# Attention decode with a gated feed-forward: w_down with 26 row slots on all partitions, and 256 rows placed apart

## The chip, the cores and the metric

The kernel runs on one core of one Trainium2 chip. The metric is the device time of one execution in microseconds (us). Three executions of the kernel before took 1341.16, 1340.95 and 1341.06 us, a median of 1341.06 us.

## The reference, cut to what matters

Two branches work on the same four vectors `x` (4 x 1024) and are mixed by a gate.

```python
q = (x @ wq)                                   # 4 x 32 heads x 128
scores = einsum("bhqd,bhkd->bhqk", q, k_cache) * 128 ** -0.5
o = einsum("bhqk,bhkd->bhqd", softmax(scores), v_cache)
a = o @ wo                                     # wo: 4096 x 1024
h = silu(x @ w_gate) * (x @ w_up)              # w_gate, w_up: 1024 x 3584
y = h @ w_down                                 # w_down: 3584 x 1024
b = x + sigmoid(x @ w_r) * y
g = sigmoid((x * gate_w).sum(-1))
out = g * a + (1 - g) * b                      # 4 x 1024
```

`k_cache` and `v_cache` hold 4 x 32 x 8192 x 128 values in bf16, 268 MB each. They are read once and used once. With the weights 575.68 MB come out of HBM.

## The kernel before

Everything that is streamed goes through one SBUF tile, `ring`, of 11 units per partition (`flat`, L173). `plan` (L177) is a list, written out by hand, of the place at which each load begins. A load is issued on SyncE's queue (SP) as soon as TensorE has read what stood in its place, so SP's order is the order of the program, and each issue waits for a count of TensorE's matmuls.

The order of the work is: `wq` (queries), `w_gate`, then 32 pairs of K blocks (`k_pair`) and 32 pairs of V blocks (`v_pair`); the V pair d - 8 follows the K pair d. One pair is 8 MB, 64 KB on each partition. VectorE transposes a K pair (L511), TensorE multiplies (L516); after eight K pairs a softmax runs over the scores, GpSimd and ScalarE spread the probabilities out (`spread_p`, L568 and L570), and TensorE multiplies them with the V pairs (L587). `w_up` is loaded and used after the second K pair, and there `h_done` (L375) makes the hidden vector h and turns it so that it can be multiplied with `w_down`. After the last K pair comes `wd_piece` (L404): it loads `w_down` and accumulates its product. Eight V pairs and `wo` follow, in pieces that become smaller towards the end (L681 to L692), and the result is stored.

`w_down` has 3584 rows of 1024 values (2 KB a row), 28 for each of the 128 partitions. Before, 27 of them lie on every partition (`FI = 27`, one transfer, L409, 54 KB a partition). The last 128 rows lie apart: 120 rows on 24 partitions, five rows on each (two transfers, L411, to the partitions 0 to 11 and 32 to 43), and eight rows on eight partitions (L412, 64 to 71). The part of the source for one L411 transfer is three groups of four runs that do not follow each other in memory, because the two transfers take their runs in turn (`e h o s`).

h has to match this placing. Its first 3456 entries (`hT`) come by eight transposes (L382) and eight multiplications (L385). For the rows apart (`hS`), ScalarE brings the entries into the order of the partitions (L392, `hp`), eleven small matmuls turn them (L397, L399), and VectorE multiplies with the gate (L402). `gu_piece` (L364) orders the columns of `w_gate` and `w_up` to match; for the last group of columns it uses two matmuls, of 3 and of 1 columns per row of the placing (L372).

Queues that matter below: SP issues all loads; GpSimd issues none; each transfer is divided among the 16 DMA engines.

Of the kernel before, what the change touches and what calls it, by code (L numbers as in the profile page):

```python
# [112 lines left out]
def kernel(  # L113
# [29 lines left out]
    ND = Bn * H // NQ  # L143
# [5 lines left out]
    FR = 4  # L149
    FG = F // (P * FR)  # L150
    NB = 512
# [10 lines left out]
    const = ctx.enter_context(tc.tile_pool(name="const", bufs=1))  # L162
# [26 lines left out]
    def turned(rows, n, dtype=BF, lo=0):  # L189
        t = TB[tb_turn[0] % 2]  # L190
        tb_turn[0] += 1
        return t[lo:lo + rows, 0:n] if dtype == BF else t[lo:lo + rows, 0:2 * n].bitcast(dtype)

    def load_pair(src, n, cuts=(1, 1), second=None):

        place, down = next(plan)
        lo = place * UN
        if second is None:
            second = place * UN + n if place + 4 <= NU else 0
        at = [lo, second]  # L200
        assert second or (n == RING and lo + n == NU * UN and not down)
        halves = [flat[:, x:x + n] for x in at]
        if cuts == (1, 1) and second == lo + n:
            nc.sync.dma_start(out=flat[:, lo:lo + 2 * n], in_=src)
        else:
            for i, half in enumerate(halves):
                step = n // cuts[i]
                for x in range(0, n, step):
                    nc.sync.dma_start(out=half[:, x:x + step], in_=src[:, i * n + x:i * n + x + step])
        return halves, list(range(RD))[::-1] if down else list(range(RD))  # L210
# [26 lines left out]
    row = const.tile([P, 2, 32], F32)  # L237
    nc.gpsimd.memset(row[:, 0, 0:1], 0.0)
    n = 1
# [19 lines left out]
    for half in range(2):  # L259
        for e in range(2):  # L260
            nc.gpsimd.tensor_copy(out=R[:, 2 * half + e].rearrange("p (n j) -> p n j", n=4),
                                  in_=ident[:, 64 * half + e:64 * half + 64:2].unsqueeze(1).to_broadcast([P, 4, 32]))
# [24 lines left out]
    c12 = const.tile([P, 2, Bn], F32)  # L287
# [32 lines left out]
    TW = DT // 2  # L320


    FI = FG * FR - 1
    FB = P * FI
    SX = 5
    wdv = B_w_down[0:FB].rearrange("(f i) n -> f (i n)", f=P)
    wd_apart = B_w_down[FB:FB + 24 * SX].rearrange("(e h o s) n -> h e o (s n)", e=3, h=2, o=4)
    wd_rest = B_w_down[FB + 24 * SX:F]
    hp = const.tile([P, 2, SX, 3, 4], F32)
    hS = const.tile([72, SX, Bn], BF)  # L330
    cS = const.tile([72, SX, Bn], F32)
    nc.gpsimd.memset(cS[:], 0.0)
    wov = A_wo.rearrange("(g p r) n -> p g r n", p=P, r=FR)

    def x_rows(ps, ws, nb, cols):
# [28 lines left out]
    def gu_piece(view, w_i):  # L364

        ws, _ = load_pair(view.rearrange("(c t) f -> c (t f)", t=DT), TW * F)

        def cols(w, t, i):
            row = w[:, t * F:t * F + FB].rearrange("p (f m) -> p f m", m=FI)
            if i < FG - 1:  # L370
                return [(0, FR, row[:, :, FR * i:FR * i + FR])]
            return [(0, FR - 1, row[:, :, FR * i:FI]), (FR - 1, FR, w[:, t * F + FB:(t + 1) * F])]  # L372
        x_rows(o_ps[w_i], ws, FG, cols)

    def h_done():  # L375
        h = turned(P, 1024, F32).rearrange("p (z n) -> p z n", z=2)
        nc.scalar.activation(out=h, in_=o_ps[0][:], func=ACT.Silu)
        nc.vector.tensor_tensor(out=h, in0=h, in1=o_ps[1][:], op=ALU.mult)
        for z in range(2):
            ht = bank(o_ps[z], 0, [FR, 4, 32])  # L380
            for r in range(FR):
                nc.tensor.transpose(out=ht[:, r].rearrange("p k i -> p (k i)"), in_=h[:, z, r:512:FR], identity=ident[:])  # L382
            kn = min(4, FG - 4 * z)
            for r in range(FR):
                nc.vector.tensor_tensor(out=hT[:, 4 * z:4 * z + kn, r, :], in0=ht[:, r, 0:kn, 0:Bn],  # L385
                                        in1=c12[:, 1:2, :].to_broadcast([P, kn, Bn]), op=ALU.mult)


        strip = slice(32 * ((FG - 1) % 4), 32 * ((FG - 1) % 4) + 32)
        tail = h[strip, 1, FR - 1:NB:FR]  # L390
        for u in range(2):
            nc.scalar.copy(out=hp[strip, u], in_=tail[:, 0:24 * SX].rearrange("p (e h o s) -> p h s e o", e=3, h=2, o=4)[:, u])  # L392
        hs_ps = bank(o_ps[0], 1, [SX, Bn])
        pick = ident[strip, strip.start:strip.start + Bn]
        for u in range(2):
            for v in range(SX):
                nc.tensor.matmul(hs_ps[32 * u:32 * u + 12, v], lhsT=hp[strip, u, v].rearrange("p e o -> p (e o)"), rhs=pick,  # L397
                                 start=True, stop=True, skip_group_check=True)
        nc.tensor.matmul(hs_ps[64:72, 0], lhsT=tail[:, 24 * SX:P], rhs=pick, start=True, stop=True, skip_group_check=True)  # L399
        for lo, m, n in ((0, 12, SX), (32, 12, SX), (64, 8, 1)):  # L400
            nc.gpsimd.tensor_copy(out=cS[lo:lo + m, 0:n], in_=c12[lo:lo + m, 1:2, :].to_broadcast([m, n, Bn]))
        nc.vector.tensor_tensor(out=hS[:], in0=hs_ps[0:72], in1=cS[:], op=ALU.mult)  # L402

    def wd_piece():  # L404
        lo = next(plan)[0] * UN
        assert (FI + SX) * D == 2 * RING and lo + 2 * RING <= NU * UN
        w = flat[:, lo:lo + 2 * RING]
        at = FI * D
        nc.sync.dma_start(out=w[:, 0:at], in_=wdv)  # L409
        for u in range(2):  # L410
            nc.sync.dma_start(out=w[32 * u:32 * u + 12, at:at + SX * D], in_=wd_apart[u])  # L411
        nc.sync.dma_start(out=w[64:72, at:at + D], in_=wd_rest)  # L412
        parts = [(hT[:, i // FR, i % FR, :], w[:, i * D:(i + 1) * D]) for i in range(FI)]
        parts += [(hS[:, v, :], w[0:72, at + v * D:at + (v + 1) * D]) for v in range(SX)]
        for i, (lhsT, rows) in enumerate(parts):
            for n in range(NH):
                mm_acc(n, lhsT, rows[:, n * NB:(n + 1) * NB], start=(i == 0))
# [54 lines left out]
    def flush_sums():  # L472
        while full:
            full.pop(0)()
# [19 lines left out]
    def k_pair(d):  # L494
        g, t = divmod(d, GD)
        Z = Zt[d % 2]
        if d == 0:
            spread(0)
        if t == 0:
            S_ps[g] = S0  # L500
        sps = S_ps[g]
        ks, order = load_pair(kv_view(A_k_cache, d), RING)
        flush_sums()
        for k, n in enumerate(order):
            unit = ks[n // JT][:, (n % JT) * UN:(n % JT + 1) * UN]
            kn = unit.bitcast(U32).rearrange("p (j h i) -> p h j i", j=CJ, h=2)
            T = unit.rearrange("p (j h i e) -> p h j i e", j=CJ, h=2, e=2)
            s = QP - 1 - (RD * t + n)
            for half in range(2):
                step = 2 * k + half  # L510
                nc.vector.transpose(out=kn[:, half], in_=kn[:, half])  # L511
                if step < 2 and ahead:
                    ahead.pop(0)()
                for e in range(2):
                    for z in range(4):
                        nc.tensor.matmul(sps[:, z, :], lhsT=Z[:, 2 * half + e, s:s + P], rhs=T[:, half, 16 * z:16 * z + 16, :, e],  # L516
                                         start=(t + k + half + e == 0),
                                         stop=(t == GD - 1 and k == RD - 1 and half + e == 2))
                if step == RD and d + 1 < ND:
                    spread(d + 1)  # L520
                if step == RD:
                    flush()
                if step == RD + 2:
                    flush_late()
        if t == GD - 1:
            ahead.extend(softmax(g))
            while g > 0 and ahead:
                ahead.pop(0)()
# [199 lines left out]
```

## Time and profile before

| what | value |
|---|---|
| time, median of three runs | 1341.06 us |
| span of the profiled execution | 1339.2 us |
| the rest of the time, outside the span (median less span) | 1.9 us |
| mean granted TensorE clock | 0.901 |
| HBM read | 575.68 MB, 430 GB/s over the span |
| share of the span in which DMA packets of SP's queue ran (16 engines) | 99.6% |
| TensorE, VectorE, ScalarE, GpSimd busy | 77%, 48%, 4%, 5% |
| w_down: main transfer issued | 1111.0 us |
| first matmul with w_down | 1141.33 us, after 5.55 us of waiting for the transfer |
| store of the result issued | 1336.83 us |

The span is counted from the first instruction to the last. The profile has no execution time of its own for this execution beside its span; the median of the runs less the span is 1.9 us, and what is worked out on the span is carried over to the median unchanged. The busy share of an engine is of little use here: with the DMA engines at 99.6%, an engine that waits is waiting for data.

### The profile page before, as it was taken

What the parts mean: (1) busy time and instruction counts of PE and PEld (TensorE: products, weight loads), DVE (VectorE), ACT (ScalarE), POOL (GpSimd) and SP (SyncE); (2) the same over time, 40 slices, a digit from 0 to 9 for tenths busy, and PEclk for the clock granted to TensorE, in tenths of its full rate; (3) what the DMA queues carried; (4) which work ended last, traced back from release to release, by engine and by line L of the source; (5) the groups of instructions that cost most, each with busy time, mean ns of one, the idle gap of its engine ahead of it and who ended that gap; (6) DMA issues with size and microseconds to landing.
All of it is one profiled execution on the core that took longest, in us unless ns stands there. A gap on an engine that the chain in (4) does not pass through costs nothing.

```text
span 1339.2 us, 6936 instructions
## 1 busy us (share of the span) xinstructions
PE 1031.3 (77%) x4654; PEld 139.8 (10%) x1486; DVE 638.7 (48%) x385; ACT 57.7 (4%) x58; POOL 67.0 (5%) x174
## 2 busy tenths in 40 slices
PE   2386787887777788777787977777797778687887
PEld 0011000001010010101001110100111011111111
DVE  2285998556553436555352556634345556100001
ACT  0000000100010000100010000100000000110000
POOL 2000000100010000100010000100001000100000
PEclk9697998898888998888889988888998889689999
DMA  9999999999999999999999999999999999999998
GB/s 415 433 437 437 435 437 435 420 438 433 433 435 437 427 433 435 429 438 431 433 431 433 435 439 427 429 433 435 438 430 428 433 429 429 438 429 445 422 422 352
DMA packets 13032, 576.14 MB, mean 430 GB/s; under 512 B 1436, under 2 KB 1700, under 8 KB 1970
## 3 DMA queue, kind: packets, MB, share of 16 engines
q1 hardware_dynamic: 12994, 575.69, 99.6%
q8 instruction: 24, 0.39, 0.1%
q14 instruction: 6, 0.05, 0.0%
q10 hardware_dynamic: 8, 0.00, 0.0%
HBM read 575.68 MB, written 0.01 MB: 430 GB/s over the span
## 4 chain that ended last, share of the span: by engine, by line
DMA 67%; PE 22%; DVE 9%; POOL 0%; ACT 0%; issue 0%; SPq 0%
DMA ring<-in_A_k_cache_dram 53%; PE S_ps L516 15%; DMA ring<-in_A_v_cache_dram 10%; DVE ring L511 9%; PE o_ps L587 5%; DMA ring<-in_B_w_gate_dram 3%; DMA ring<-in_A_wo_dram 2%; PE o_ps L342 1%; POOL PB L570 0%; DVE mx L536 0%; PE led L633 0%; ACT TB L545 0%; PE acc L296 0%; POOL Z L492 0%; PE o_ps L633 0%
## 5 line engine op out<-in xcount | busy, mean ns | idle before, releaser
L511 DVE STREAM_TRANSPOSE ring<-ring 128x2048 uint32<-128x2048 uint32 x256 | 566.5, 2276 | 307.7 <-DMA ring<-in_A_k_cache_dram 307.7
L516 PE MATMUL S_ps<-ring,Z 128*128 128x512 bf16 x2048 | 519.9, 408 | 229.3 <-DVE ring L511 216.1
L587 PE MATMUL o_ps<-ring,PB 128*64 128x512 bf16 x2048 | 457.4, 384 | 35.7 <-DMA ring<-in_A_v_cache_dram 33.3
L516 PEld LDWEIGHTS <-Z 128*128 128x128 bf16 x512 | 53.0, 104 | 683.0 <-issue 683.0
L617 DVE SCALAR_TENSOR_TENSOR OS<-o_ps,mE,OS 128x512 f32<-128x512 f32 x33 | 24.8, 751 | 161.7 <-ACT OS L613 160.2
L587 PEld LDWEIGHTS <-PB 128*64 128x64 bf16 x512 | 56.7, 111 | 428.3 <-issue 427.6
L625 DVE SCALAR_TENSOR_TENSOR OS<-o_ps,mE,OS 128x512 f32<-128x512 f32 x5 | 3.7, 750 | 143.6 <-ACT OS L623 143.6
L492 POOL COPY Z<-qa 32x4 bf16<-32x4 bf16 x128 | 25.8, 201 | 716.7 <-PE S_ps L516 689.6
L570 POOL COPY PB<-PT 32x1024 bf16<-32x1024 bf16 (+3 forms) x23 | 33.4, 1452 | 466.6 <-PE o_ps L587 360.7
L613 ACT ACTIVATE OS<-o_ps,mE 128x512 f32<-128x512 f32 x11 | 7.6, 687 | 671.2 <-PE o_ps L587 671.2
L568 ACT COPY PB<-PT 32x1024 bf16<-32x1024 bf16 (+3 forms) x21 | 30.3, 1444 | 22.4 <-PE o_ps L587 17.4
L545 ACT ACTIVATE TB<-S_ps,mx 128x2048 bf16<-128x2048 f32 x4 | 7.9, 1967 | 321.7 <-DVE mx L542 321.7
L254 PE MATMUL S_ps<-identb,x 6*128 6x6 bf16 x8 | 0.6, 196 | 22.3 <-DMA x<-in_gate_w_dram 22.3
L342 PE MATMUL o_ps<-ring,xw 128*4 128x512 bf16 (+2 forms) x128 | 12.9, 490 | 3.5 <-DMA ring<-in_B_w_gate_dram 3.5
L633 PEld LDWEIGHTS o_ps<-selg,OS 128*128 128x128 f32 x88 | 11.5, 191 | 8.8 <-issue 8.5
L550 DVE STREAM_TRANSPOSE PT<-TB 128x2048 bf16<-128x2048 bf16 x4 | 9.2, 2312 | 6.4 <-ACT TB L545 6.4
L296 PE MATMUL acc<-ring,hT 128*4 128x512 bf16 x54 | 7.9, 466 | 5.5 <-DMA ring<-in_B_w_down_dram 5.5
L536 DVE TENSOR_REDUCE mx<-S_ps 128x1 f32<-128x2048 f32 x4 | 9.1, 2282 | 6.0 <-PE S_ps L516 6.0
L296 PE MATMUL acc<-ring,LT 128*4 128x512 bf16 x64 | 8.8, 378 | 3.3 <-DMA ring<-in_A_wo_dram 2.8
L633 PE MATMUL o_ps<-selg,OS 128*128 128x8 f32 x88 | 10.5, 245 | 0.0
L623 ACT ACTIVATE OS<-o_ps,mE 128x512 f32<-128x512 f32 x5 | 3.4, 687 | 151.2 <-PE o_ps L587 151.2
L256 DVE COPY xw<-S_ps 128x48 bf16<-128x48 bf16 x1 | 0.2, 184 | 17.5 <-PE S_ps L254 17.5
(83 smaller groups left out, 88.4 us busy)
## 6 DMA issues: line engine op xcount, KB each, us to landing
ring<-in_A_v_cache_dram SPq DMA_DIRECT2D x7, 4096.0 KB
ring<-in_A_k_cache_dram SPq DMA_DIRECT2D x6, 4096.0 KB, 33.9
ring<-in_A_v_cache_dram SPq DMA_DIRECT2D x6, 2048.0 KB, 28.9
ring<-in_B_w_gate_dram SPq DMA_DIRECT2D x1, 7168.0 KB
ring<-in_B_w_up_dram SPq DMA_DIRECT2D x1, 7168.0 KB
ring<-in_B_w_down_dram SPq DMA_DIRECT2D x1, 6912.0 KB
ring<-in_A_wo_dram SPq DMA_DIRECT2D x2, 2048.0 KB
ring<-in_A_wo_dram SPq DMA_DIRECT2D x3, 1024.0 KB, 34.5
```

Of the source, the lines that this page charges most:

```text
L296: nc.tensor.matmul(acc(n), lhsT=lhsT, rhs=rhs, start=start, stop=True, skip_group_check=True)
L342: nc.tensor.matmul(ps[32 * k:32 * k + Bn, z, :].rearrange("p (f r) -> p f r", r=FR)[:, :, lo:hi], lhsT=xT[TW * half + t], rhs=rhs, start=( ...
L492: nc.gpsimd.tensor_copy(out=Z[at, :, QP - 1 + QP * q], in_=qa[at, :, h0 + q, b])
L511: nc.vector.transpose(out=kn[:, half], in_=kn[:, half])
L516: nc.tensor.matmul(sps[:, z, :], lhsT=Z[:, 2 * half + e, s:s + P], rhs=T[:, half, 16 * z:16 * z + 16, :, e], start=(t + k + half + e == 0) ...
L536: nc.vector.tensor_reduce(out=mx[:, 0:1], in_=sps[:].rearrange("p z n -> p (z n)"), axis=AX.X, op=ALU.max)
L550: nc.vector.transpose(out=PT[:].rearrange("p j i -> p (j i)"), in_=PTs)
L568: nc.scalar.copy(out=Bv[at, :, :, q, :], in_=Pv[at])
L570: nc.gpsimd.tensor_copy(out=Bv[at, :, :, q, :], in_=Pv[at])
L587: nc.tensor.matmul(o_ps[w // 2][row:row + NM, w % 2, :], lhsT=PB[:, RD * (d % NW) + n, z].rearrange("p w s j -> p (w s j)"), rhs=vn[:, j0 ...
L617: nc.vector.scalar_tensor_tensor(out=OS[:], in0=o_ps[w // 2][:, w % 2, :], scalar=mE[:, w:w + 1], in1=OS[:], op0=ALU.mult, op1=ALU.add)
L633: nc.tensor.matmul(oT, lhsT=OS[:, q * Dh:(q + 1) * Dh], rhs=selg[:, q].rearrange("p t s -> p (t s)"), start=(q == 0), stop=(q == 3), skip_ ...
```

## The change

Of the 28 rows that fall to a partition, 26 instead of 27 are placed on every partition (`FI = FG * FR - 2`). So 256 rows lie apart instead of 128, in a list `apart`, whose entries are first partition, e, o, rows per partition, and queue:

- partitions 0 to 11, six rows each (72 rows), and 32 to 43, five rows each (60 rows), on SP's queue;
- partitions 64 to 77, one row each (14), 88 to 95, six rows each (48), 12 to 25, one row each (14), and 120 to 127, six rows each (48), on GpSimd's queue.

GpSimd issued no transfer before. Each source is now a run of rows that follow each other in memory, seen as `(e o s)`. In the built program the transfers stand as 12x6144 and 12x5120 on SP, and 14x1024, 8x6144, 14x1024 and 8x6144 on GpSimd; before they stood as 12x1x5120 (twice) and 8x1024 on SP.

The loads are taken out of `wd_piece` into `wd_load`, which is called in the last K pair just after that pair's own load. SP's order stays as it was. On GpSimd the four transfers come after the copies of L492 for the last K pair and before the copies of L570 for the last softmax.

`hS` now has all 128 partitions and six places, with zeros where no row lies. `h_done` takes a second buffer of TB, clears 768 values on 32 partitions of it on GpSimd, and has seven copies on ScalarE instead of two, 24 small matmuls instead of eleven, and no copies of the gate on GpSimd. The products with the rows apart read 128 partitions instead of 72, in six steps instead of five; 26 and 6 make the same 32 steps as 27 and 5.

```diff
-    FI = FG * FR - 1
+    FI = FG * FR - 2
     FB = P * FI
-    SX = 5
+    FT = F - FB
+    SX = 6
-    wd_apart = B_w_down[FB:FB + 24 * SX].rearrange("(e h o s) n -> h e o (s n)", e=3, h=2, o=4)
-    wd_rest = B_w_down[FB + 24 * SX:F]
-    cS = const.tile([72, SX, Bn], F32)
+    apart = [(0, 3, 4, 6, nc.sync), (32, 3, 4, 5, nc.sync), (64, 14, 1, 1, nc.gpsimd), (88, 2, 4, 6, nc.gpsimd),
+             (12, 14, 1, 1, nc.gpsimd), (120, 2, 4, 6, nc.gpsimd)]
...
-            return [(0, FR - 1, row[:, :, FR * i:FI]), (FR - 1, FR, w[:, t * F + FB:(t + 1) * F])]
+            n = FI - FR * i
+            return [(0, n, row[:, :, FR * i:FI]), (n, FR, w[:, t * F + FB:(t + 1) * F].rearrange("p (r f) -> p f r", f=P))]
...
+        hx = turned(P, FT + P * SX, F32)
+        nc.gpsimd.memset(hp, 0.0)
+        nc.scalar.copy(out=tail.rearrange("p (r f) -> p r f", f=P), in_=...)
+        for lo, e, o, s, _ in apart:
+            nc.scalar.copy(out=hp[:, lo // 32, 0:s, lo % 32:lo % 32 + e * o], in_=...)
...
+    def wd_load():
...
         nc.sync.dma_start(out=w[:, 0:at], in_=wdv)
-        for u in range(2):
-            nc.sync.dma_start(out=w[32 * u:32 * u + 12, at:at + SX * D], in_=wd_apart[u])
-        nc.sync.dma_start(out=w[64:72, at:at + D], in_=wd_rest)
+        x = FB
+        for lo, e, o, s, queue in apart:
+            src = B_w_down[x:x + e * o * s]
+            src = src if s == 1 else src.rearrange("(e o s) n -> e o (s n)", e=e, o=o)
+            queue.dma_start(out=w[lo:lo + e * o, at:at + s * D], in_=src)
+            x += e * o * s
...
         ks, order = load_pair(kv_view(A_k_cache, d), RING)
+        if d == ND - 1:
+            wd_load()
```

More of the change, by code (lines that the diff above doesn't have):

```diff
@@ L320 @@
     TW = DT // 2
-    FI = FG * FR - 1
+    FI = FG * FR - 2
     FB = P * FI
-    SX = 5
+    FT = F - FB
+    SX = 6
     wdv = B_w_down[0:FB].rearrange("(f i) n -> f (i n)", f=P)
-    wd_apart = B_w_down[FB:FB + 24 * SX].rearrange("(e h o s) n -> h e o (s n)", e=3, h=2, o=4)
-    wd_rest = B_w_down[FB + 24 * SX:F]
-    hp = const.tile([P, 2, SX, 3, 4], F32)
-    hS = const.tile([72, SX, Bn], BF)
-    cS = const.tile([72, SX, Bn], F32)
-    nc.gpsimd.memset(cS[:], 0.0)
+    apart = [(0, 3, 4, 6, nc.sync), (32, 3, 4, 5, nc.sync), (64, 14, 1, 1, nc.gpsimd), (88, 2, 4, 6, nc.gpsimd),
+             (12, 14, 1, 1, nc.gpsimd), (120, 2, 4, 6, nc.gpsimd)]
+    assert sum(e * o * s for _, e, o, s, _ in apart) == FT
+    hS = const.tile([P, SX, Bn], BF)
     wov = A_wo.rearrange("(g p r) n -> p g r n", p=P, r=FR)
@@ L389, in h_done @@
         strip = slice(32 * ((FG - 1) % 4), 32 * ((FG - 1) % 4) + 32)
-        tail = h[strip, 1, FR - 1:NB:FR]
-        for u in range(2):
-            nc.scalar.copy(out=hp[strip, u], in_=tail[:, 0:24 * SX].rearrange("p (e h o s) -> p h s e o", e=3, h=2, o=4)[:, u])
+        hx = turned(P, FT + P * SX, F32)
+        tail, hp = hx[strip, 0:FT], hx[strip, FT:FT + P * SX].rearrange("p (j s m) -> p j s m", j=4, s=SX)
+        nc.gpsimd.memset(hp, 0.0)
+        nc.scalar.copy(out=tail.rearrange("p (r f) -> p r f", f=P), in_=h[strip, 1].rearrange("p (f r) -> p r f", r=FR)[:, FR - FT // P:FR])
+        x = 0
+        for lo, e, o, s, _ in apart:
+            nc.scalar.copy(out=hp[:, lo // 32, 0:s, lo % 32:lo % 32 + e * o], in_=tail[:, x:x + e * o * s].rearrange("p (m s) -> p s m", s=s))
+            x += e * o * s
         hs_ps = bank(o_ps[0], 1, [SX, Bn])
         pick = ident[strip, strip.start:strip.start + Bn]
-        for u in range(2):
+        for j in range(4):
             for v in range(SX):
[L397 to L404, printed above, removed]
+                nc.tensor.matmul(hs_ps[32 * j:32 * j + 32, v], lhsT=hp[:, j, v], rhs=pick, start=True, stop=True, skip_group_check=True)
+        nc.vector.tensor_tensor(out=hS[:], in0=hs_ps, in1=c12[:, 1:2, :].to_broadcast([P, SX, Bn]), op=ALU.mult)
+    wd = []
+    def wd_load():
         lo = next(plan)[0] * UN
@@ L407, in wd_piece @@
         w = flat[:, lo:lo + 2 * RING]
+        wd.append(w)
         at = FI * D
         nc.sync.dma_start(out=w[:, 0:at], in_=wdv)
-        for u in range(2):
-            nc.sync.dma_start(out=w[32 * u:32 * u + 12, at:at + SX * D], in_=wd_apart[u])
-        nc.sync.dma_start(out=w[64:72, at:at + D], in_=wd_rest)
+        x = FB
[3 more added lines that the diff above has]
+            queue.dma_start(out=w[lo:lo + e * o, at:at + s * D], in_=src)
+            x += e * o * s
+    def wd_piece():
+        w = wd[0]
+        at = FI * D
         parts = [(hT[:, i // FR, i % FR, :], w[:, i * D:(i + 1) * D]) for i in range(FI)]
-        parts += [(hS[:, v, :], w[0:72, at + v * D:at + (v + 1) * D]) for v in range(SX)]
+        parts += [(hS[:, v, :], w[:, at + v * D:at + (v + 1) * D]) for v in range(SX)]
         for i, (lhsT, rows) in enumerate(parts):
```

## The prediction

> **What bounds the kernel now.** I read the page's queues first, then transfers by stretch of time, then the timeline around w_down, then the last microseconds.
>
> ```profile
> span 1339.2 us, 6936 instructions
> DMA  9999999999999999999999999999999999999998
> q1 hardware_dynamic: 12994, 575.69, 99.6%
> q8 instruction: 24, 0.39, 0.1%
> SPq L204 <- PE S_ps L516: 572.6, 29, 26.2
> ```
>
> SP's queue (q1) keeps the 16 DMA engines busy for 99.6% of the span. SP's waits show that loads wait for TensorE to free the ring; but in the trace every load up to the last is issued at least 3.4 us before the first engine has finished the one ahead of it, so no engine runs dry. The end is therefore the end of the last of 16 DMA engines, and a change counts by what it adds to or takes from the latest ones. q8 fetches instructions, 24 times 16 KB.
>
> The stretch from 1330 us to 1340 us, in slices of 0.25 us:
>
> ```profile
> DMA  9999976966668766554541000000000000100000
> q1 hardware_dynamic: 623, 1.51, 38.4%
> ```
>
> The digits fall from 9 to 4 between 1331 and 1335.5 us: the engines don't finish together. The landing records of the last wo transfer give all 16 ends: four engines at 1331.24 to 1331.93, four at 1334.20 to 1334.76, eight at 1335.57 to 1335.98 us. After the last, 3.2 us remain to the span's end (matmul, cast, store), which the change leaves alone. Were all engines level, they would end some 1.6 us earlier (mean of the 16 ends against 1335.98), which caps the gain of any redistribution.
>
> What one engine does in a unit of time, from two stretches of 1.9 us (30.4 engine-us), the first without an instruction fetch, the second with one:
>
> ```profile
> q1 hardware_dynamic: 11, 0.72, 87.6%
> ```
> ```profile
> q1 hardware_dynamic: 15, 0.98, 121.2%
> q8 instruction: 1, 0.02, 3.3%
> ```
>
> Eleven packets of 64 KB take 26.6 us, 2.42 us each, 0.038 us a KB. With a fetch, the 15 packets take 36.8 us instead of 36.3, and the fetch 1.0 us, though 16 KB are worth 0.61. So a visit to another queue costs its engine 1.55 us, 0.94 beyond its bytes. The landings agree: around three fetches the engine concerned falls back by 1.54 to 1.56 us against the others.
>
> Around w_down:
>
> ```profile
> 1111.00 0.33 SPq L409 DMA_DIRECT2D ring<-in_B_w_down_dram  x1
> 1113.16 1.61 SPq L411 DMA_DIRECT2D ring<-in_B_w_down_dram  x2
> 1114.82 0.44 SPq L412 DMA_DIRECT2D ring<-in_B_w_down_dram  x1
> ```
> ```profile
> 1067.12 0.96 POOL L492 COPY Z<-qa 32x4 bf16<-32x4 bf16 x4 [37.69 <-PE S_ps L516]
> 1143.54 4.88 POOL L570 COPY PB<-PT 32x768 bf16<-32x768 bf16 x3 [75.46 <-DVE PT L550]
> ```
> ```profile
> 1141.33 7.95 PE L296 MATMUL acc<-ring,hT 128*4 128x512 bf16 x54 [5.55 <-DMA ring<-in_B_w_down_dram]
> ```
>
> Landing records tell on how many engines a transfer runs: each L411 transfer (three groups of four runs) landed on three, L412 (eight rows) on eight, the load of x (four rows) on four. The main transfer landed on seven engines at 1136.4 to 1137.1 us and on nine at 1139.5 to 1141.3. L411's three are among the seven early ones: they took its 80 KB (3 us) and thereby joined the late. Four early engines were left, and they are the four that end first.
>
> **The change, part by part.**
>
> *Main transfer, 26 slots:* 8 rows of 2 KB less on every engine, -16 KB, -0.60 us on all.
>
> *The rows apart on SP.* The intention reads (3 groups, 4 partitions): three engines. But the source runs now follow each other, and the built program has 12 rows of 6144 and of 5120 elements, with no groups. By the rows for L412 and x (as many engines as rows) each goes to 12 engines, 12 + 10 = 22 KB on each. Twelve of 16 engines cannot avoid the eight that end last: at least four of these get it, +0.83 us. The three that carried 80 KB get 58 KB less, which nobody needs. L412 falls away: -2 KB on eight engines.
>
> *The rows apart on GpSimd:* 248 KB, by the same rows on 14, 8, 14 and 8 engines; which ones no row shows. An engine gets 0 to 28 KB, 15.5 on average. A sum by bytes for a late engine: -16 - 1 (half of L412's 2) + 22 + 15.5 = about +20 KB, +0.8 us; bounds +3 to +34 KB, so +0.1 to +1.3.
>
> *The second queue.* In the stretch of these transfers the engines run nothing but q1 before; now each of the four GpSimd transfers turns up on an engine that is in the middle of q1's packets. No row shows GpSimd's queue. Bounds: 0, if the engine slips the other packet in as smoothly as the next of its own (these start within some ns of the one before); 0.94 us a visit, as for a fetch, which is the only second queue that the trace shows beside q1, and so the value I take. Visits: 14 + 8 + 14 + 8 = 44 over 16 engines, 2.75; an engine that is late and unlucky has three (four at most). 3 x 0.94 = +2.8 us. GpSimd issues the four one after another and the engines' packets then last 1.2 us (32 KB), so I count the visits apart; two that fall together would save 0.94.
>
> *GpSimd's wait.* The first and second issue wait for TensorE as L409 and L411 do (1111 to 1113 us). Behind them on GpSimd stands L570, which starts at 1143.54. Four issues of 1 to 2 us (SP takes 0.3 to 0.9; my estimate is double) end by 1121: 22 us to spare. The data is needed at 1141, behind the main transfer. 0 us; without this cover L570 would delay the first V pair.
>
> *SP's issues:* three instead of four after the K load, 9 to 23 us ahead of need: 0.
>
> *h_done,* at 104 to 108 us:
>
> ```profile
> 107.68 0.17 DVE L402 TENSOR_TENSOR hS<-o_ps,cS 72x20 bf16<-72x20 f32 x1 [0.35 <-PE o_ps L399]
> 115.22 6.70 DVE L511 STREAM_TRANSPOSE ring<-ring 128x2048 uint32<-128x2048 uint32 x3 [7.37 <-DMA ring<-in_A_k_cache_dram]
> ```
>
> Five more ScalarE copies at 0.25 us (two took 0.49), the first longer, 13 more matmuls of some 0.04 us, a clearing on GpSimd under 1 us that can run earlier: +2 to +3 us, inside the 7.37 us in which VectorE waits for the third K pair. 0. Without that cover, up to 3 us in the loads' lead of 9 us, still 0.
>
> *gu_piece* has as many matmuls of the same 512 columns; *wd_piece* has the same 64 matmuls, of which twelve instead of ten read the rows apart: 0, for TensorE waits for data on both sides (5.55 us before, 9.46 after).
>
> Sum: +0.8 + 2.8 = **+3.6 us**. Span 1339.2 + 3.6 = 1342.8; with the 1.9 us outside it 1344.7 us.
>
> **Rivals.**
>
> *Smooth change of queue (not slower).* Place: the engines at 1112 to 1120 us. If a visit costs only bytes, the end moves by +0.1 to +1.3: 1341.9. For it: packets within q1 follow without a gap, and GpSimd's are small (2 and 12 KB). Against: q8. It decides from under 0.63 us a visit at three visits, (2.7 - 0.8) / 3. Measurements of this kernel tell about 0.2% (2.7 us) from no change. [...]
>
> *The placing works as it reads (faster).* 88 KB on three early engines and 96 KB on two more early ones, whose 4 us of lead cover 80 KB more (3.0 us); all others lose 16 KB and take 4: -12 KB, -0.45 us, 1340.6. Against: the merged sources. It needs smooth visits too.
>
> *More visits.* If each GpSimd transfer also visits every engine for its completion, apart from its data, an engine has up to seven visits: 6.6 + 0.8 = +7.4, 1348.5. Against: SP's transfers on fewer engines show landings only on these. [...]
>
> *Fetches.* 13 more matmuls shift TensorE's code; one fetch more or on another late engine is 1.55 us either way. It stays in the range.
>
> **How the numbers follow.** Forecast (two to four full visits, +2.7 to +5.1 with the bytes) 0.50; smooth visits 0.31; placing as it reads 0.07; more visits 0.12. Predicted 1344.7. The range reaches from 1341.2 (smooth, least bytes, 1341.06 + 0.1) to 1347.1 (five visits and 1.3 us of bytes, +6.0), leaving out the placing and most of the last case; the forecast's own is 1343.8 to 1346.2. Slower by over 0.2% (above 1343.74): the forecast and the last, 0.61 after a little off for its lower edge and a little on for an unlucky fetch. Faster by over 0.2% would need 2.7 us where level engines would give 1.6: 0.02. Within: 0.37.
>
> **What would show it.** GpSimd's queue as a line of its own in the list of queues, and its four issues near 1111 to 1121 us. L419 on SP landing on 12 engines; if on three, my reading of the merged source is wrong. q1 packets of 3 instead of 2.42 us next to GpSimd's, if visits cost; if they keep 2.42, the forecast falls to +0.8. The last landing at 1339 to 1340 us instead of 1335.98, all engines shifted alike by the visits, and the four early ones still early. The first w_down matmul at 1143 to 1145 us. VectorE's third K pair still waiting for its load. Wrong also if the loads' lead of 3.4 us is used up somewhere, or if the queue of GpSimd costs time at the start.

## The result, and the profile after

| | median of five runs | lowest and highest |
|---|---|---|
| before | 1341.16 us | 1340.95 to 1341.31 |
| after | 1349.89 us | 1349.03 to 1350.64 |

The ratio is 1.0064 (95% interval 1.0052 to 1.0075): 8.7 us slower. The direction was forecast, the size was not: 1344.7 us was predicted, with a range up to 1347.1. The profiled execution took 1349.03 us, 1.9 us more than its span. It is the fastest of the five: its span is 7.9 us longer than that of before, and this is what the account below explains. No trace shows where the further 0.8 us of the median come from.

The page of the changed kernel, first the span, then how busy the DMA engines were in 40 slices, what they moved, and the queues:

```profile
span 1347.1 us, 6996 instructions
...
DMA  9999999999999999999999999999999999999998
GB/s 416 450 431 421 432 437 434 431 432 434 436 432 434 436 431 432 429 434 436 434 428 436 436 434 431 428 432 432 429 433 435 434 427 366 422 422 439 433 417 338
...
q1 hardware_dynamic: 12996, 575.44, 99.4%
...
q0 software_dynamic: 128, 0.25, 0.1%
```

GpSimd's queue has a line of its own, q0, with 128 packets and 0.25 MB. The row of busy tenths shows nothing at all: it is nine in every slice but the last, as before. The row of GB/s below it does: the 34th slice (1111 to 1145 us) has 366 GB/s, where its neighbours have 427 and 422. The engines' digit is 9 there as well, but they move less.

The timeline around the transfers and the points that the prediction named (start, duration, engine, line, what, in brackets the idle time before it and what ended it):

```profile
109.90 0.18 DVE L404 TENSOR_TENSOR hS<-o_ps,c 128x24 bf16<-128x24 f32 x1 [1.69 <-PE o_ps L403]
115.04 4.50 DVE L525 STREAM_TRANSPOSE ring<-ring 128x2048 uint32<-128x2048 uint32 x2 [4.96 <-DMA ring<-in_A_k_cache_dram]
...
1110.17 0.33 SPq L414 DMA_DIRECT2D ring<-in_B_w_down_dram  x1
1110.88 0.64 POOL L419 DMA_DIRECT2D ring<-in_B_w_down_dram  x1 [43.00 <-PE o_ps L601]
1112.76 0.73 SPq L419 DMA_DIRECT2D ring<-in_B_w_down_dram  x2
1113.03 1.54 POOL L419 DMA_DIRECT2D ring<-in_B_w_down_dram  x3 [1.51 <-PE o_ps L601]
...
1147.53 7.30 PE L296 MATMUL acc<-ring,hT 128*4 128x512 bf16 x52 [6.50 <-DMA ring<-in_B_w_down_dram]
1148.79 4.88 POOL L584 COPY PB<-PT 32x768 bf16<-32x768 bf16 x3 [34.22 <-DVE PT L564]
```

GpSimd has issued its four transfers by 1114.57 us and waits 34 us before its next copies; `hS` is done at 110 us and VectorE still waits 4.96 us for the third K pair. Neither is late. The first matmul with w_down starts at 1147.53 us, 6.2 us later than before.

Where the time went is told by the transfers in two stretches of time. Before, 1111 to 1132 us and then 1132 to 1150 us:

```profile
DMA packets 246, 9.20 MB, mean 438 GB/s; under 512 B 25, under 2 KB 25, under 8 KB 25
...
DMA packets 184, 7.79 MB, mean 433 GB/s; under 512 B 30, under 2 KB 30, under 8 KB 38
```

The same two stretches of the changed kernel:

```profile
DMA packets 343, 7.65 MB, mean 364 GB/s; under 512 B 109, under 2 KB 109, under 8 KB 137
...
q1 hardware_dynamic: 215, 7.39, 97.3%
q0 software_dynamic: 128, 0.25, 4.9%
...
DMA packets 175, 6.62 MB, mean 368 GB/s; under 512 B 40, under 2 KB 40, under 8 KB 40
...
q1 hardware_dynamic: 174, 6.61, 102.5%
```

(The share of a queue adds up the time of all packets that start in the stretch, over the time of 16 engines, so it can exceed 100%.)

In the first, beside GpSimd's packets, 1.55 MB less were moved, worth 3.5 us at 0.438 MB a us. In the second no packet of GpSimd's queue is left, and still 1.17 MB are missing, 2.7 us. This second hole lies where SP's two transfers to the rows apart run. Beyond their bytes (+0.83 us) no term of the prediction stood for it.

The packet records allow a finer count. An undisturbed packet costs 2.42 us per 64 KB; what a packet takes beyond that, summed over the data packets of SP's and GpSimd's queues and divided by 16, is the **excess** per engine. It is used for all runs below.

- Before: 0.06 us per engine in the first stretch, 0.12 in the second.
- After: 3.7 us in the first (53.4 engine-us in SP's packets, 6.1 in GpSimd's own). Some 85 of SP's packets are stretched: packets of 32 KB, worth 1.21 us, take up to 1.6 us longer.
- After: 3.2 us in the second (50.7 engine-us, 64 packets; 64 KB packets take up to 2.7 us longer).

3.7 + 3.2 and the predicted 0.8 us of bytes make 7.7 us. The last landing of the last wo transfer moved by 7.8 us, from 1335.98 to 1343.80 us, the first from 1331.24 to 1337.72 us. In order of their ends the 16 engines finished 5.6 to 7.9 us later, 6.8 us on average. Both kernels move the same bytes in all, so the average is lost time, and it is the excess (6.9 us, less the 0.2 us of before): no engine ran dry for long.

### The profile page after: what moved, and what is told of

Its sections match the earlier page's. It is cut to its first block, busy times and chain, and to the rows that moved or that the text cites. A ratio compares the mean times of both kernels' runs of the same rounds, so it can differ in the third digit from the quotient of the medians.

```text
span 1347.1 us, 6996 instructions
## 1 busy us (share of the span) xinstructions
PE 1040.4 (77%) x4680; PEld 143.2 (11%) x1512; DVE 638.7 (47%) x385; ACT 59.0 (4%) x63; POOL 69.0 (5%) x175
## 4 chain that ended last, share of the span: by engine, by line
DMA 67%; PE 22%; DVE 10%; ACT 0%; issue 0%; SPq 0%; DVEq 0%
DMA ring<-in_A_k_cache_dram 52%; PE S_ps L530 15%; DMA ring<-in_A_v_cache_dram 11%; DVE ring L525 10%; PE o_ps L601 5%; DMA ring<-in_B_w_gate_dram 3%; DMA ring<-in_A_wo_dram 2%; PE o_ps L342 1%; PE led L647 0%; DVE OS L631 0%; DVE mx L550 0%; ACT TB L559 0%; PE acc L296 0%; DVE OS L639 0%; ACT OS L637 0%
## 5 line engine op out<-in xcount | busy, mean ns | idle before, releaser
L530 PE MATMUL S_ps<-ring,Z 128*128 128x512 bf16 x2048 | 525.6, 412 | 225.8 <-DVE ring L525 217.9
L584 POOL COPY PB<-PT 32x1024 bf16<-32x1024 bf16 (+3 forms) x23 | 33.4, 1450 | 428.4 <-PE o_ps L601 363.5
L342 PE MATMUL o_ps<-ring,xw 128*4 128x512 bf16 (+1 forms) x128 | 12.8, 461 | 4.6 <-DMA ring<-in_B_w_gate_dram 4.6
```

Source lines behind the costliest of these rows:

```text
L342: nc.tensor.matmul(ps[32 * k:32 * k + Bn, z, :].rearrange("p (f r) -> p f r", r=FR)[:, :, lo:hi], lhsT=xT[TW * half + t], rhs=rhs, start=( ...
L584: nc.gpsimd.tensor_copy(out=Bv[at, :, :, q, :], in_=Pv[at])
```

## The experiments

Two theories stood at first. **The queue** (Q): an engine that turns to GpSimd's queue and back loses time, as the prediction had it. **Crowding** (C): engines that write into partitions that other engines are writing at the same moment slow each other, whichever queue brings the packet. No record tells which engine writes which partitions of a large transfer; where an expectation says that engines serve or own partitions, that is part of C, assumed by the author and not shown. SP's second hole speaks against Q as the only cause; the first hole fits both.

**e1: all six transfers on SP's queue.**

```diff
-    apart = [(0, 3, 4, 6, nc.sync), (32, 3, 4, 5, nc.sync), (64, 14, 1, 1, nc.gpsimd), (88, 2, 4, 6, nc.gpsimd),
-             (12, 14, 1, 1, nc.gpsimd), (120, 2, 4, 6, nc.gpsimd)]
+    apart = [(0, 3, 4, 6, nc.sync), (32, 3, 4, 5, nc.sync), (64, 14, 1, 1, nc.sync), (88, 2, 4, 6, nc.sync),
+             (12, 14, 1, 1, nc.sync), (120, 2, 4, 6, nc.sync)]
```

> The changed kernel with all six transfers of rows apart on SP's queue; placing, sources and arithmetic as in the changed kernel, which is 8.7 us slower than the one before. Its trace has two stretches in which SP's packets take longer than their size explains: 1113 to 1132 us beside GpSimd's transfers (3.7 us for each engine) and 1137.5 to 1148 us, where SP's own two transfers of rows apart run and no GpSimd packet is left (3.2 us for each engine). Theory Q (the second queue costs): the first stretch goes, the kernel is 4 to 5 us slower than before. Theory C (crowding: a transfer whose engines are more than those that serve its partitions in a 128-partition transfer holds these engines up): the rows of the two 8x6144 transfers crowd as before, only on SP, so it stays 6 to 8 us slower, and packets after the main w_down transfer are stretched by 5 to 7 us for each engine.

Measured: 1348.56 us against 1341.28, ratio 1.0056 (1.0041 to 1.0071). There is no q0, and the slowness stays. It has moved: the first stretch is clean, the second holds all of it, because SP's transfers run behind the main one.

```profile
DMA packets 248, 9.13 MB, mean 435 GB/s; under 512 B 25, under 2 KB 25, under 8 KB 25
...
DMA packets 230, 5.05 MB, mean 281 GB/s; under 512 B 84, under 2 KB 84, under 8 KB 112
...
q1 hardware_dynamic: 228, 5.03, 102.6%
```

The excess is 0.06 us per engine and then 6.8, as much as both holes of the changed kernel together (6.9). Which queue carries the rows does not matter; Q falls as the main cause.

**e2: the kernel before, with the sources of its two transfers merged.** The 60 rows of each L411 transfer follow each other in memory, and so the three groups vanish, as they do in the change. Slots, queue and target partitions stay those of before.

```diff
-    wd_apart = B_w_down[FB:FB + 24 * SX].rearrange("(e h o s) n -> h e o (s n)", e=3, h=2, o=4)
+    wd_apart = [B_w_down[FB + 12 * SX * u:FB + 12 * SX * (u + 1)].rearrange("(e o s) n -> e o (s n)", e=3, o=4) for u in range(2)]
...
-            nc.scalar.copy(out=hp[strip, u], in_=tail[:, 0:24 * SX].rearrange("p (e h o s) -> p h s e o", e=3, h=2, o=4)[:, u])
+            nc.scalar.copy(out=hp[strip, u], in_=tail[:, 12 * SX * u:12 * SX * (u + 1)].rearrange("p (e o s) -> p s e o", e=3, o=4))
```

> The kernel before; only the two transfers L411 take their 60 rows as one run of memory each, so that the built source has 12 rows instead of 3 groups of 4, and the order of the entries of h follows. GpSimd has no transfer. By bytes, twelve engines get 20 KB (0.76 us) and three lose 60 KB: +0.8 us. Theory C: 12 engines write to the partitions 0 to 11 and 32 to 43, which three engines serve in the main transfer: +0.8 and about 3 us more, 3.5 to 4.5 us slower than before, with stretched packets of 10 KB and of the main transfer's end. Theory Q: no second queue, +0.8 us, no packet stretched.

Measured: 1345.7 us, ratio 1.0033 (1.0021 to 1.0046), so +4.4 us from the order of rows in memory alone. Each transfer landed on twelve engines instead of three; so not every transfer is divided among all 16 engines (before, the main transfer landed on 16, each L411 transfer on three, L412 on eight). The second stretch has the hole, though q1 is the only queue with data:

```profile
DMA packets 188, 6.87 MB, mean 382 GB/s; under 512 B 48, under 2 KB 48, under 8 KB 56
...
q1 hardware_dynamic: 187, 6.85, 102.4%
```

The excess is 2.6 us per engine. With the 0.8 us of bytes that makes the 3.3 us by which the profiled execution is longer (a span of 1342.5 us against 1339.2); it is the fastest of six, 1.3 us below their median. The same 24 partitions get the same bytes from twelve engines instead of three; theory C puts the excess down to that.

**e3: the kernel before, with four small transfers on GpSimd's queue** (14 rows of 256 bytes each, into a tile that is not read any more; all else as before).

```diff
+        if d == ND - 1:
+            for i in range(4):
+                nc.gpsimd.dma_start(out=spare[32 * i:32 * i + 14], in_=B_w_down[14 * i:14 * i + 14, 0:128])
```

> The kernel before, with four transfers more, on GpSimd's queue, of 14 rows of 256 bytes each into 14 partitions of a tile that is no longer used; they are issued at about 1068 us and nobody waits for them. They leave the placing of w_down alone and add 14 KB in all. Theory Q: each engine is visited by each transfer, for data and for the completion: as in the changed kernel's first stretch, 3 to 4 us slower (0.94 us for each of 4 visits). Theory C: next to nothing is moved, so at most 0.5 us slower.

Measured: 1341.43 us against 1341.28, ratio 1.0 (0.9991 to 1.001). The transfers of 1068 to 1092 us:

```profile
DMA packets 304, 10.50 MB, mean 438 GB/s; under 512 B 144, under 2 KB 144, under 8 KB 144
...
q1 hardware_dynamic: 176, 10.49, 101.2%
q0 software_dynamic: 128, 0.01, 0.4%
```

128 packets of q0, as many as in the change, and none of SP's packets is stretched. Turning to the second queue costs nothing that can be measured; the 0.94 us a visit is refuted.

**e4: the changed kernel, with SP's two transfers again as three groups** (their source rows lie 44 apart, so they can't merge); GpSimd's stay.

```diff
-    apart = [(0, 3, 4, 6, nc.sync), (32, 3, 4, 5, nc.sync), (64, 14, 1, 1, nc.gpsimd), (88, 2, 4, 6, nc.gpsimd),
-             (12, 14, 1, 1, nc.gpsimd), (120, 2, 4, 6, nc.gpsimd)]
+    apart = [(0, 3, 4, 6, nc.sync, 0, 44, 0), (32, 3, 4, 5, nc.sync, 0, 44, 24), (64, 14, 1, 1, nc.gpsimd, 132, 1, 0),
+             (88, 8, 1, 6, nc.gpsimd, 146, 6, 0), (12, 14, 1, 1, nc.gpsimd, 194, 1, 0), (120, 8, 1, 6, nc.gpsimd, 208, 6, 0)]
...
+            src = B_w_down[FB + x:FB + x + e * g].rearrange("(e k) n -> e k n", e=e)[:, off:off + o * s]
```

> The changed kernel; only the two SP transfers of rows apart take their rows in three groups of 44 (24 for the first, 20 for the second), so that the built source keeps three groups and each transfer should land on three engines, 88 KB on each. GpSimd's four transfers as in the changed kernel. Theory C: the second stretch (3.2 us for each engine) goes, and 0.8 us of bytes on the late engines: 4 to 5 us slower than before. Theory Q: only the bytes go, 7 to 8 us slower than before.

Measured: 1345.41 us, ratio 1.003 (1.0019 to 1.0041): half of the loss is gone. Both transfers landed on three engines. The hole beside GpSimd's packets stays, SP's is closed:

```profile
DMA packets 340, 7.47 MB, mean 356 GB/s; under 512 B 109, under 2 KB 109, under 8 KB 137
...
DMA packets 180, 8.02 MB, mean 446 GB/s; under 512 B 22, under 2 KB 22, under 8 KB 22
```

The excess is 4.0 and 0.08 us per engine (SP's packets alone have 3.6 in the first, the figure that later expectations use). So the two holes are separate and add up.

**e5: GpSimd's two large transfers in groups as well** (two groups of four partitions; the rest as in e4).

```diff
-             (88, 8, 1, 6, nc.gpsimd, 146, 6, 0), (12, 14, 1, 1, nc.gpsimd, 194, 1, 0), (120, 8, 1, 6, nc.gpsimd, 208, 6, 0)]
+             (88, 2, 4, 6, nc.gpsimd, 160, 48, 0), (12, 14, 1, 1, nc.gpsimd, 146, 1, 0), (120, 2, 4, 6, nc.gpsimd, 160, 48, 24)]
```

> The changed kernel with groups kept in all four large transfers of rows apart: three groups on SP as in e4_groups_sp, and two groups of four partitions for the two 8x6144 transfers of GpSimd (rows of 48, 24 for each transfer). [...] Theory C (crowding): the stretch of 3.6 us for each engine beside GpSimd's transfers shrinks to under 0.5 us, and the kernel is between 0.5 us faster and 0.7 us slower than before. Theory C-HBM (engines that read neighbouring rows at the same time are slow, whatever they write): GpSimd's two groups read 12 KB runs that lie 48 rows apart, so it improves too, and this run can't tell it from C. Theory G (GpSimd's queue with large rows costs, crowded or not): still 3 to 4.5 us slower, as e4_groups_sp.

Measured: 1345.31 us against 1341.07, ratio 1.0031 (1.002 to 1.0042). A miss: no better than e4.

```profile
DMA packets 397, 8.38 MB, mean 399 GB/s; under 512 B 152, under 2 KB 152, under 8 KB 180
...
q0 software_dynamic: 166, 0.19, 3.0%
```

399 GB/s is better than 356, but not the 438 of before: an excess of 2.5 us per engine, and 0.4 more behind 1132 us, where GpSimd's packets go on. There are 180 packets of four bytes instead of 84, and the 12 KB packets don't come as eight together any more: the first eight start in four pairs, the others singly, 1.2 to 1.5 us apart. This reads as if GpSimd executed each of the two transfers in four pieces (3 pieces more, 2 transfers and 16 engines make the 96 further packets). Grouping did not act on GpSimd's queue (2.5 us left of e4's 4.0) as on SP's (0.08 us left of 3.2 in e4). Which engines ran the pieces, and into which partitions, the records don't show; so e5 decides nothing between the theories.

**e6: e1's six transfers, with target partitions four apart,** so that no small set of neighbouring partitions is filled.

The list is that of first partition, step, partitions, rows and queue:

```diff
+    apart = [(0, 4, 12, 6, nc.sync), (1, 4, 12, 5, nc.sync), (2, 4, 14, 1, nc.sync), (64, 4, 8, 6, nc.sync),
+             (3, 4, 14, 1, nc.sync), (65, 4, 8, 6, nc.sync)]
...
+            queue.dma_start(out=w[lo:lo + step * (m - 1) + 1:step, at:at + s * D],
+                            in_=B_w_down[x:x + m * s].rearrange("(m s) n -> m (s n)", s=s))
```

> The kernel of e1_all_sp (six merged transfers, all on SP, on 12, 12, 14, 8, 14 and 8 engines, the same rows of the source read in the same way), but the destinations lie four partitions apart: 0, 4, ... 44 and so on, instead of next to each other. Theory C (crowded destinations): the stretch of packets, 6.8 us for each engine in e1_all_sp, falls to 0.5 to 2 us, and the kernel is 1 to 3 us slower than before instead of 7.3. Theory C-HBM (neighbouring rows read by many engines): nothing changes, 7 us slower.

Measured: 1359.78 us, ratio 1.0137 (1.0123 to 1.0151). The time can't be used: the spaced targets made the last K pair's work wait for these transfers.

```profile
1143.04 17.66 DVE L527 STREAM_TRANSPOSE ring<-ring 128x2048 uint32<-128x2048 uint32 x8 [38.68 <-DMA ring<-in_B_w_down_dram]
1145.40 12.86 PE L532 MATMUL S_ps<-ring,Z 128*128 128x512 bf16 x48 [25.16 <-DVE ring L527]
```

VectorE waited 38.68 us for w_down's transfers before it could go on with the last K pair, TensorE stood still for 25.16 us, the next V load was issued at 1151 instead of 1123 us, and the DMA engines ran dry (only 2.60 MB between 1132 and 1150 us). The excess fell from e1's 6.8 to 0.8 us per engine, which fits crowding, but with no V load beside the transfers it is no proof. A spaced placing without that wait was not tried.

**e7: the kernel before, with the 27th slot of all 128 partitions on GpSimd's queue:** 256 KB, about as much as the change gives to it, but spread over all partitions.

```diff
-        nc.sync.dma_start(out=w[:, 0:at], in_=wdv)
+        nc.sync.dma_start(out=w[:, 0:at - D], in_=wdv[:, 0:at - D])
...
+            nc.gpsimd.dma_start(out=wd[0][:, (FI - 1) * D:FI * D], in_=wdv[:, (FI - 1) * D:FI * D])
```

> The kernel before; only the 27th row slot of all 128 partitions (128 rows, 256 KB) is taken out of the main transfer and loaded by one transfer of GpSimd's queue, issued after the last K pair's load. [...] Theory C (only destinations that crowd cost): within 0.5 us of before, and no packet of SP's stretched by more than 0.3 us beside GpSimd's. Theory G (GpSimd's queue costs as soon as it carries real rows): 1 to 4 us slower, since the changed kernel and e4_groups_sp lose 3.6 us for each engine with 248 KB on that queue.

Measured: 1341.37 us against 1341.05, ratio 1.0004 (0.9995 to 1.0013). The stretch of 1111 to 1132 us:

```profile
DMA packets 325, 9.19 MB, mean 438 GB/s; under 512 B 41, under 2 KB 41, under 8 KB 105
...
q1 hardware_dynamic: 245, 8.93, 98.8%
q0 software_dynamic: 80, 0.26, 3.1%
```

0.26 MB of q0 and a full 438 GB/s; none of SP's packets is stretched. So it is not the bytes on GpSimd's queue either. What is left is where they go, and the size of the packets (4 KB here, 2 and 12 KB in the change); the next runs hold the size fixed.

**e8: the kernel before, with the rows apart on other partitions.** Same source rows, same three groups, again three engines, same queue; only the targets are 64 to 75 and 96 to 107 (and 0 to 7 for the eight single rows).

```diff
-            nc.sync.dma_start(out=w[32 * u:32 * u + 12, at:at + SX * D], in_=wd_apart[u])
-        nc.sync.dma_start(out=w[64:72, at:at + D], in_=wd_rest)
+            nc.sync.dma_start(out=w[64 + 32 * u:64 + 32 * u + 12, at:at + SX * D], in_=wd_apart[u])
+        nc.sync.dma_start(out=w[0:8, at:at + D], in_=wd_rest)
```

> [...] All on SP. Theory C: the three engines now share the way into these partitions with their owners for 80 KB each, so packets of both are stretched and the kernel is 1.5 to 4 us slower. Theory C-HBM (what is read, and by how many engines, decides): as before, within 0.3 us.

Measured: 1344.64 us against 1341.05, ratio 1.0027 (1.0016 to 1.0037).

```profile
DMA packets 166, 6.60 MB, mean 367 GB/s; under 512 B 30, under 2 KB 30, under 8 KB 38
...
q1 hardware_dynamic: 165, 6.58, 103.5%
```

From 1132 to 1150 us 367 GB/s instead of 433, an excess of 3.4 us per engine. The reads from HBM are the same ones, so they aren't the cause; the partitions are: the same three groups have 0.12 us on 0 to 11 and 32 to 43 (before). Three engines are enough. They hold up the others too: the nine engines that end the main transfer last, none of which carries an L411 transfer (the first of these has landed on its three engines by 1141.04 us), land it at 1142.25 to 1144.72 us instead of 1139.48 to 1141.28, and of the last wo transfer all 16 landings come 3.1 to 4.0 us later, 3.4 on average.

**e9 and e10: 240 rows on five engines, to two places.** All on SP's queue, 26 slots as in the change; five groups of four partitions, six rows each, twice, and sixteen single rows. In e9 (the run on own partitions, by theory C) the groups go to 0 to 19 and 32 to 51 and the single rows to 64 to 79; in e10 (foreign partitions, by theory C) to 64 to 83, 96 to 115 and 0 to 15. Both have the same sources, and in both the two grouped transfers land on five engines.

The list of e9, which takes the place of e4's:

```diff
+    apart = [(0, 5, 4, 6, nc.sync, 0, 48, 0), (32, 5, 4, 6, nc.sync, 0, 48, 24), (64, 16, 1, 1, nc.sync, 240, 1, 0)]
```

and e10 against e9:

```diff
-    apart = [(0, 5, 4, 6, nc.sync, 0, 48, 0), (32, 5, 4, 6, nc.sync, 0, 48, 24), (64, 16, 1, 1, nc.sync, 240, 1, 0)]
+    apart = [(64, 5, 4, 6, nc.sync, 0, 48, 0), (96, 5, 4, 6, nc.sync, 0, 48, 24), (0, 16, 1, 1, nc.sync, 240, 1, 0)]
```

> [...] Crowding theory: no packet is stretched; between 1111 and 1150 us less than 0.3 us of packet time per engine beyond the bytes, as in the kernel before. The time then goes by bytes alone: -0.5 us on most engines; the two engines that newly carry 96 KB get about 80 KB net, +3.0 us, which shows only if they are among the late ones. So 1340.5 to 1344.1 us. Rival (rows apart cost by themselves, wherever they go): a stretch as in the changed kernel, 3 us per engine or more, and a time of 1344 us or more.

> [...] Tells what sets the size of the crowding. If the bytes into the fullest set of partitions count (20 partitions on each side are five sets of eight; 96 KB each): 96 x 0.038 = 3.6 us of packet time per engine beyond the bytes. If all bytes written into foreign partitions count (240 KB gave 3.4 us on three engines; here 480 KB): about 6.8 us. The time above that of the run on own partitions: +3.6 or +6.8 us. If crowding is not the cause: the same time as that run.

Measured: e9 1342.61 us against 1340.99, ratio 1.0013 (1.0004 to 1.0022); e10 1349.02 us, ratio 1.0059 (1.0047 to 1.0072). The stretch of 1132 to 1150 us, e9:

```profile
DMA packets 215, 7.68 MB, mean 426 GB/s; under 512 B 42, under 2 KB 42, under 8 KB 58
```

and e10:

```profile
DMA packets 188, 5.92 MB, mean 329 GB/s; under 512 B 42, under 2 KB 42, under 8 KB 58
```

As many packets below 8 KB, 1.76 MB less. In e9, 256 rows apart cost 1.6 us, and the excess is 0.5 us per engine, a little over the 0.3 expected; w_down's transfers to five engines have landed at 1142.88 us and the single rows at 1143.10, where before all had landed at 1141.54. So the 1.6 us are there already, and they lie on one engine: of the last wo transfer it lands at 1337.67 us, the other 15 by 1335.61, 0.4 us before the last one of the kernel before. By bytes, one of the two engines that newly carry 96 KB was not early enough.

In e10 the excess is 4.6 us per engine, between the two sizes expected (3.6 and 6.8) and nearer to the first. (No record shows that partitions count in sets; 96 KB are what each of the five engines puts on the eight partitions of its two groups.) The time above e9 is 6.4 us, more than the mean excess, because it falls unevenly: the five engines' forty 12 KB packets take 0.43 us longer each than in e9, 40 x 0.43 / 5 = 3.4 us on each of the five beside what their other packets lose. One of the five lands its rows at 1149.56 us, the other four by 1144.17; at the end the latest engine is 6.3 us behind that of e9, the average 4.3.

The excess is what moves the ends. The 16 landings of the last wo transfer came later, on average, by 6.8 us in the changed kernel and in e1, 2.5 in e2, 4.0 in e4, 2.8 in e5, 3.4 in e8, 0.4 in e9 and 4.7 in e10; the excesses are 6.9, 6.8, 2.6, 4.1, 2.9, 3.4, 0.5 and 4.6.

The table sets the excess beside the bytes of the transfers of rows apart that run in the stretch, and beside what these bytes are worth when all 16 engines share them, at 0.038 us a KB (2.42 us per 64 KB). The single rows on SP's queue in before, e8, e9 and e10 (16 to 32 KB) are not counted. e5 and e6 are left out: in e5 no record shows which engine wrote where, in e6 no V load ran beside the transfers.

| kernel and stretch | partitions | KB | KB / 16 x 0.038 | excess measured |
|---|---|---|---|---|
| before, L411 in three groups | 0 to 11, 32 to 43 | 240 | 0.6 us | 0.12 us |
| e4, SP's two in three groups | 0 to 11, 32 to 43 | 264 | 0.6 us | 0.08 us |
| e9, in five groups | 0 to 19, 32 to 51 | 480 | 1.1 us | 0.5 us |
| after, SP's two transfers, merged | 0 to 11, 32 to 43 | 264 | 0.6 us | 3.2 us |
| after and e4, GpSimd's four | 12 to 25, 64 to 77, 88 to 95, 120 to 127 | 248 | 0.6 us | 3.7 and 4.0 us |
| e1, all six behind each other | as in after | 512 | 1.2 us | 6.8 us |
| e2, merged | 0 to 11, 32 to 43 | 240 | 0.6 us | 2.6 us |
| e8, in three groups | 64 to 75, 96 to 107 | 240 | 0.6 us | 3.4 us |
| e10, in five groups | 64 to 83, 96 to 115 | 480 | 1.1 us | 4.6 us |

With 240 to 264 KB the excess is either 0.08 to 0.12 us or 2.6 to 4.0, so the bytes alone don't decide. It is small where the groups go to the partitions from 0 and from 32 on, and large where the same groups go elsewhere (e8, e10) or the same partitions are filled by twelve engines (after, e2); which engines carry GpSimd's rows is not recorded. Nor do the bytes set its size: twice as many as in e8 give 6.8 us in e1, but 4.6 in e10. In e8 engines with no part in the crowded transfer were held up as well; by what path, no run shows.

## Why the prediction was wrong

- *Main transfer, 26 slots* (-0.60 us on all): no run takes it apart, and none speaks against it (in e9, 15 of 16 engines end by 1335.61 us, where before the last ended at 1335.98).
- *The rows apart on SP go to twelve engines:* right; twelve landings each. But only their bytes were counted, +0.83 us. That twelve write into partitions that in the kernel before get their rows from three (three landings) cost 3.2 us per engine on top. The prediction had read the merged source correctly and drew the smaller of its two consequences.
- *The rows apart on GpSimd,* bytes: the sum of +0.8 us fits what is left of the 7.8 us when the excess is taken off (0.9). In e4, where SP's rows are back on three engines, the same terms give -16 - 1 + 15.5 = -1.5 KB, and nothing is left: the last landing moved by 4.0 us, the excess is 4.1. (The lower bound adds up to -16 - 2 + 22 = +4 KB, not +3, which changes nothing.)
- ***The second queue*, 3 x 0.94 = +2.8 us: this is the step that failed.** Its mechanism is refuted: 128 packets of q0 cost nothing in e3, and 256 KB on that queue nothing in e7. The 0.94 us was taken from instruction fetches, the only second queue in the trace; why a fetch costs it stays open, but a turn to GpSimd's queue does not cost it. The step that should have stood there is a different one, crowding of target partitions, and it has two terms: 3.7 us beside GpSimd's transfers and 3.2 us beside SP's, 6.9 instead of 2.8. Runs e1, e2, e8 and e10 show it on SP's queue alone. That the kernel came out slower, as forecast, is luck: with the queue's term at nothing the prediction's own sum is +0.8 us.
- *GpSimd's wait* (0), *SP's issues* (0), *h_done* (0): right. GpSimd issued from 1110.88 to 1114.57 us, 0.5 to 0.6 us each, 34 us ahead of L584; the third K pair still waited 4.96 us.
- *gu_piece, wd_piece* (0): nothing in the trace against it; TensorE still waits for data on both sides of w_down's matmuls, 6.50 us ahead of them (5.55 before) and 10.21 us behind them (9.46 before). The work ahead of them also ended later, at 1141.03 instead of 1135.78 us (start less wait).
- *Signs:* the four issues came at 1111 to 1115 us, as foretold; the last landing was foretold for 1339 to 1340 us and came at 1343.80; w_down's first matmul for 1143 to 1145 and came at 1147.53. The four early engines don't stand apart any more: the 16 ends lie between 1337.72 and 1343.80 us with no gap above 1.2 us. "q1 packets of 3 instead of 2.42 us next to GpSimd's" was seen in kind (32 KB packets of up to 2.8 us instead of 1.21), and would have been taken for a proof of the wrong mechanism, had the second hole not stood beside it.
- *Rival "smooth change of queue":* right on the queue, wrong on the time, since crowding came on top. *Rival "more visits":* its 1348.5 us is nearest to the result, by the wrong reason. Its condition holds in the trace: each of the four GpSimd transfers landed 16 times, though they have 14 or 8 rows. But their 84 four-byte packets took 9 ns each (median), 1.0 engine-us in all; no run shows that such a visit costs 0.94 us. A number near the result is no evidence for its mechanism. *Rival "the placing works as it reads":* in e9, with rows apart in groups on five engines (0 to 19 and 32 to 51), the time is 1.6 us above that of before, so the further engines chosen there aren't all early, and nothing was gained; the rival's own placing, 88 and 96 KB on five engines, was not reached, since e5 did not keep GpSimd's groups.

What stays open: which engine writes which partitions in the main transfer, and so why some targets stretch packets and others don't; why grouped transfers on GpSimd's queue (e5) still stretch packets; and what exactly sets the size of the excess (e10).

## What to carry to other kernels

When a kernel is bound by its DMA engines, as this one is (q1 at 99.6%), count a transfer to a few partitions twice: by the bytes that each engine gets, and by the partitions they are written to. Here 240 to 264 KB, worth 0.6 us if all 16 engines share them, cost next to nothing in one placing (0.12 us per engine before, 0.08 in e4) and 2.6 to 4.0 us in others (after, e2, e4's GpSimd rows, e8). A source that merged into one run lost its groups here, with no change in bytes: twelve landings instead of three, and 4.4 us (e2). Look at the shape in the built program and at the number of landings.

To find it, don't look at how busy the DMA engines are: in the 34th slice of the changed kernel the busy digit is 9, with 366 GB/s, for a stretched packet counts as busy. Look for a dip in GB/s, and then for packets longer than others of their size (here 32 KB packets of up to 2.8 us instead of 1.21).

## What the hardware showed unexpectedly

- The second queue cost nothing by itself: 128 packets of GpSimd's queue amid SP's, ratio 1.0 (0.9991 to 1.001), and 256 KB over all partitions, 1.0004 (0.9995 to 1.0013).
- The same bytes and rows on the same queue, on three engines both times, cost 3.6 us more when written to other partitions (e8).
- Engines without a part in the small transfer were held up too: in e8 three engines carried it, 59 packets were stretched by over 0.1 us between 1132 and 1150 us, those of the main transfer and of the V load among them, and all 16 engines ended 3.1 to 4.0 us later.
- Two grouped transfers on GpSimd's queue took 96 more four-byte packets than ungrouped ones, and their rows no longer went out together (e5).
